# The division of a strip put ahead of the next strip's pass, the first loads reordered, the means of v behind the first scores

## The chip, the cores and the metric

One core of a Trainium2 chip runs the kernel. The metric is the device time of one execution in microseconds (us), the median of several runs.

## The reference

Windowed attention with block summaries, then two feed-forward layers on the same 1536 tokens (width 512, inner width 2048), all in float32.

```python
k_sum = k.reshape(B, H, nb, 32, D).max(axis=3)      # B=2 H=8 S=768 D=64 nb=24
v_sum = v.reshape(B, H, nb, 32, D).mean(axis=3)
scores_l = where(|i-j| < 16, scale * q @ k.T, -1e9)
scores_s = scale * einsum(q, k_sum) + log(32)
a = exp(concat(scores_l, scores_s) - rowmax)
a = a / (a.sum() + 1e-09)
x = a @ concat(v, v_sum)                             # -> 1536 x 512
g = max(h, 0) + alpha * min(h, 0),  h = x @ w_in     # layer 1
x = g @ w_out
g = P(h) / (Q(h) + 1e-6),  h = x @ w_in              # layer 2, P cubic, Q quadratic in |h|
out = g @ w_out
```

## The kernel before

The attention goes over 24 strips of 64 query rows (12 for each batch element). A strip needs 96 keys of its neighbourhood and 24 block maxima, so its score tile `s` is 128 x 4 x 120: two heads on the partitions, four head pairs beside each other. Its steps are small functions, and each has a short name in the tables below:

- `in` loads the strip's queries (`qz`, 256 KB), `v` its values (`vc`, 192 KB); `k` copies its keys out of the half of k that was loaded as a whole (`kt`) into `kc`; `ks` adds the block maxima `kmax`, `vm` the block means `vmean`.
- `qk` (line 394, TensorE) makes the scores; `mask` (402, VectorE) adds the bias, `max` (410, VectorE) finds the row extreme.
- `exp` (420, 424, ScalarE) has two forms, chosen for each strip by `SOFTMAX`: four activations that also add up the row ("a"), or one wide one ("s") after `sub` (415, GpSimd) with `sum` (429, VectorE) behind it.
- `guard` (434, 436) adds 1e-9 to the sum, `inv` (440, VectorE) takes the reciprocal, `norm` (444, VectorE or GpSimd) multiplies. `turn` (450, TensorE) transposes, `turned` copies the result `pT`, `pv` (464, TensorE) multiplies with the values into `po`, `out` and `outl` (478, VectorE) split `po` into a high part `xh` and a rest `xl`.

The feed-forward layers run each product as three TensorE passes of high and low parts (lines 195 and 258). Their weights come as raw words (`raw`, 1 MB each, two buffers) and are split by ScalarE (`top`, line 161), VectorE (`cv`, 163), ScalarE again (`wih`, `woh`) and GpSimd (`wil`, `wol`, line 173). Layer 1 of the first tokens starts while the attention still runs: its first product `h` is in pass 6 and needs strips 0 to 3.

The order is written out by hand. A loop over passes t = -1 to 27 (lines 576 to 622) goes through one of the strings in `ORDERS`; `PHASES = (3, 5, 7, 10, 14)` says which: the first for t < 3, the second for t = 3, 4, the third for 5, 6, the fourth for 7 to 9, the fifth for 10 to 13. In pass t `qk`, `mask` and `max` serve strip t, `exp`, `sum`, `guard`, `inv` and `norm` strip t-1, `turn` strip t-2, `pv` and `out` strip t-3, `k` strip t+1. Every engine works off its instructions strictly in that order. `ENG` names the engine of a step in each of the six phases (a ScalarE, v VectorE, p GpSimd). `FIRST` is the order of the loads before the loop. `VMEAN_AT` gives the pass in which each 128 rows of v enter the block means (`att_vmean`, line 359, TensorE, tile `vps`), `VLOAD_T` the pass from which the rows of the second batch element are loaded, `KMAX_AT` and `KLOAD_AT` the same for the block maxima and loads of k of the second element. All loads are issued by SyncE, in order; each waits until the load eight places ahead of it has landed, and where it fills a buffer again also for that buffer's readers. `na` and `ab` are the coefficients of layer 2.

From pass 10 on, and in all that follows, the order is not touched by the change.

Of the kernel before, what the change touches and what calls it, by code (L numbers as in the profile page):

```python
# [31 lines left out]
N_FIRST = 3  # L32
EARLY = 8

VMEAN_AT = (-1, -1, 0, 0, 1, 2, 6, 7, 8, 9, 9, 9)
VLOAD_T = 3
KMAX_AT = (3, 3, 3, 6, 9, 9, 9, 10)
KLOAD_AT = (2, 7)
WLOAD_AT = (1, 2)

PHASES = (3, 5, 7, 10, 14)
ORDERS = (
    ("qk mask k act mid exp max turn gl vmean sum kmax vm end ks out hi low pv inv sub outl Y norm guard turned "
     "v act in act H gh new"),
    ("act qk sum hi mid turn act vm act mask in exp vmean gh gl max pv ks v guard out inv sub low turned k end Y "
     "outl kmax H new norm"),
    ("qk vm exp hi act mask pv mid sum max out Y turn sub inv gl guard in low outl act v vmean k act norm H "
     "turned new ks end kmax gh"),
    ("gh qk act pv ks act act exp out end mask hi k sum gl max vmean outl low kmax turn guard mid Y v vm in sub "
     "inv new turned H norm"),  # L50
    ("ks act end act gh exp qk pv hi out mid v act mask k sum gl max outl sub turn vmean Y kmax low H turned in "
     "new inv vm guard norm"),
    ("vm act act gh act qk exp mask hi sum max pv gl inv sub out k mid v outl in turn turned vmean kmax new low "
     "guard ks Y end H norm"),
)

FIRST = 'k0 v0 v1 k1 q0 q2 v2 v3 q1'

SOFTMAX = 'aaaassasaasssabssssssass'

ENG = {"guard": "vapppv", "k": "vaaaaa", "turned": "aaaaaa", "vm": "aaapaa", "ks": "ppppav", "norm": "vppppp", "sub": "pppppp",
       "gl": "vvvppp", "gh": "vapaaa", "hi": "vaaaaa", "mid": "pvpppp", "end": "pppppp", "out": "aaaaaa", "al": "vavaaa"}

LEAD = (4, 6, 4, 4, 9, 13, 5, 10)
# [6 lines left out]
def kernel(  # L71
# [59 lines left out]
    def eng(step):  # L131
        return {"a": nc.scalar, "v": nc.vector, "p": nc.gpsimd}[ENG[step][sum(now[0] >= t for t in PHASES)]]

# [9 lines left out]
    def w_load(layer, nm, j):  # L143
        raw = rawp.tile([P, 4160], I16, tag="raw", name="raw")
        words = src_of[layer, nm][:, 2 * j:2 * j + 2, :].rearrange("p a b -> p (a b)").bitcast(I16)
        nc.sync.dma_start(out=raw[:, 1:4097], in_=words)
        raws[layer, nm, j] = raw
        loaded[layer, nm, j] = now[0]
# [32 lines left out]
    hps, ts, gs, yps, new, count = {}, {}, {}, {}, {}, [0]  # L181
# [51 lines left out]
    def g_split(u, f):  # L233
        n, t = u[3], ts[u, f]
        gh = gp.tile([P, 512], F32R, tag="gh", name="gh")[:, :n]
        gl = gp.tile([P, 512], F32R, tag="gl", name="gl")[:, :n]
        copy("gh", gh, t)
        gs[u, f] = gh, gl

    def g_low(u, f):  # L240
        t, (gh, gl) = ts.pop((u, f)), gs[u, f]
        (eng("gl") if (u, f) != steps[-1] else nc.vector).tensor_tensor(out=gl, in0=t, in1=gh.bitcast(F32), op=ALU.subtract)  # L242
# [66 lines left out]
    for e in range(3):  # L309
        t = a1.tile([P, KEYS], F32, name=f"bias{e}")  # L310
# [21 lines left out]
    kt, kmax, vt, vmean, st = {}, {}, {}, {}, {}  # L332

    def att_load(b, half):
        pool = e1 if (b, half) == (0, 1) else ktp
        kt[b, half] = pool.tile([P, NPAIR, HALF], F32, tag="kt", name="kt")
        for hp in range(NPAIR):
            nc.sync.dma_start(out=kt[b, half][:, hp, :], in_=kT[b, :, hp, half * (S // 2):half * (S // 2) + HALF])

    def att_kmax(b, i):  # L340
        half, hp = divmod(i, NPAIR)
        if i == 0:
            kmax[b] = a2.tile([P, NPAIR, NB], F32, tag="kmax", name="kmax")
        nc.vector.tensor_reduce(
            out=kmax[b][:, hp, half * NB // 2:(half + 1) * NB // 2],
            in_=kt[b, half][:, hp, WINDOW:WINDOW + S // 2].rearrange("p (n i) -> p n i", i=BLOCK),
            axis=AX.X, op=ALU.max)

    def att_vload(b, i):
        vt[b, i] = e1.tile([P, DM], F32, tag="vt", name="vt", bufs=NVT)  # L350
        s0 = WINDOW + i * P
        nc.sync.dma_start(out=vt[b, i], in_=vS[b, s0:s0 + P, :])

    def att_vmean(b, i):

        if i == 0:
            vmean[b] = psy.tile([P, 512], F32, tag=f"y{b}", name="vps")
        z0 = (NV - 1 - i) * (P // BLOCK)
        nc.tensor.matmul(out=vmean[b][0:KEYS, :], lhsT=mean[:, z0:z0 + KEYS], rhs=vt[b, i],
                         start=(i == 0), stop=(i == NV - 1))  # L360
        n = b * NV + i + NVT
        if n < B * NV:
            vlate.append(n)
        if i == NV - 1:
            ps, vmean[b] = vmean[b], (b1 if b else e1).tile([KEYS, DM], F32, tag=f"vmean{b}", name=f"vmean{b}")
            nc.scalar.copy(vmean[b][STRIP:KEYS, :], ps[STRIP:KEYS, :])
# [155 lines left out]
    def vmean_at(t):  # L522
        for i, at in enumerate(VMEAN_AT):
            if at == t:
                att_vmean(*divmod(i, NV))
        while vlate and (vlate[0] < NV or t >= VLOAD_T):
            att_vload(*divmod(vlate.pop(0), NV))

    def kmax_at(t):
        for i, at in enumerate(KMAX_AT):  # L530
            if at == t:
                att_kmax(1, i)
# [8 lines left out]
    def w_place(i):  # L541
        pool = ctx.enter_context(tc.tile_pool(name=f"wp{i}", bufs=1, reuse_waits="tile"))
        places.update({x: pool for x in opened[i][1]})

    def w_step(place, most=0):
        for i, (w, at, x) in enumerate(w_now):
            if at == place and (place != "hi" or x in places):
                w_now[i] = w, next(w, None), x
        w_now[:] = [x for x in w_now if x[1]]
        if len(w_now) < most and preps and preps[0] in raws and now[0] > loaded[preps[0]] + (now[0] <= LAST):  # L550
            layer, nm, j = p = preps[0]
            if now[0] >= need.get(p, 0) - LEAD[j] and now[0] + AHEAD >= opens[nm, j] and spare(*p):
                w = w_split(*preps.pop(0))
                w_now.append((w, next(w), (nm, j)))
# [13 lines left out]
    with tc.manual_schedule():  # L568
        for step in FIRST.split():
            {"k": lambda i: att_load(0, i), "v": lambda i: att_vload(0, i), "q": att_in}[step[0]](int(step[1]))  # L570
        for i in range(2 * NPAIR):
            att_kmax(0, i)
        for i, at in enumerate(VMEAN_AT):
            if at == -2:
                att_vmean(*divmod(i, NV))
        for t in range(-1, LAST + 1):
            now[0] = t
            if t == CLOSE_E:
                att_e.close()
                w_place(1)  # L580
            if t == NQ:
                att_qk.close()
                w_place(2)
            if t == 2:
                nc.sync.dma_start(out=al, in_=alpha)
                nc.sync.dma_start(out=na, in_=pa.partition_broadcast(P))
                nc.sync.dma_start(out=ab, in_=pb.partition_broadcast(P))
            if t == 5:
                nc.scalar.mul(na, na, -1.0)
                nc.scalar.activation(out=ab, in_=ab, func=AF.Abs)  # L590
            if t in KLOAD_AT:
                att_load(1, KLOAD_AT.index(t))
            act = acts.pop(0) if acts else iter(())
            g = later.pop(t, None)
            for step in ORDERS[sum(t >= at for at in PHASES)].split():
                if step in attn:
                    f, o = attn[step]
                    for n in {t + o, t + o - (o < -1)}:
                        if 0 <= n < NQ and n - t - o == -(o < -1 and n >= EARLY):
                            f(n)  # L600
                elif step in every:
                    every[step](t)
                elif step == "act":
                    next(act, None)
                elif step in ("gh", "gl"):
                    if g:
                        (g_split if step == "gh" else g_low)(*g)
                else:
                    w_step(step, 2 if step == "new" else 0)
            if t in WLOAD_AT:  # L610
                w_load(*loads.pop(0))
        for act in acts:
            for _ in act:
                pass
        for t in sorted(later):
            g_split(*later[t])
            g_low(*later[t])
# [104 lines left out]
```

## Time and profile before

| what | us |
|---|---|
| median of 3 runs | 621.86 (621.47 to 623.15) |
| the profiled execution, own time | 620.94 |
| its span | 618.8 |
| TensorE busy | 594.4 (96% of the span) |
| ScalarE, GpSimd, VectorE busy | 383.7, 354.8, 338.9 |

Some 2.1 us of the profiled execution lie outside its span. Rows of the trace give start, duration, engine, line, output, input, count, and in brackets how long the engine had been idle before and what released it. PEld are TensorE's weight loads, DVE is VectorE, ACT ScalarE, POOL GpSimd, SPq the queue of SyncE. Rows on one engine overlap by about 0.1 us, since an instruction starts while the one before it still writes.

### The profile page before, as it was taken

Reading aid. Unit: us, or ns where it says so; the run is one execution under the profiler, and the core shown is the slowest. Engines: PE = TensorE matmul, PEld = TensorE weight load, DVE = VectorE, ACT = ScalarE, POOL = GpSimd, SP = SyncE. Lnnn points to the kernel's source line nnn. Section 1 sums busy time; section 2 is a strip of 40 time slices with the busy share of each in tenths; the row PEclk is TensorE's granted clock in tenths of the full one; section 3 lists DMA queues with packets and bytes.
Section 4 is the critical chain, followed back from the end, with each engine's and each line's share of the span. In section 5 each row is a group of like instructions: output and inputs, shape, how many; then the busy total and the mean of one; then the engine's idle time right before and its main releaser. Section 6 shows DMA issues by size and latency. Waiting matters only on the chain.

```text
span 618.8 us, 8590 instructions
## 1 busy us (share of the span) xinstructions
PE 594.4 (96%) x3192; PEld 496.2 (80%) x3192; DVE 338.9 (55%) x494; ACT 383.7 (62%) x665; POOL 354.8 (57%) x343
## 2 busy tenths in 40 slices
PE   4679999999999999999999999999999999999996
PEld 2567989988888888888888888888888888888884
DVE  4766678654222111144555277776566666566664
ACT  1789798877444333367777467776566666566663
POOL 3266779675622222147777557776466666466662
PEclk9779999999999999999999999999999999999999
DMA  8898576524300000015555101000100000100001
GB/s 298 294 322 285 172 243 226 192 83 151 122 0 2 0 1 1 0 69 187 182 183 197 68 1 68 1 0 2 48 21 1 0 1 1 69 0 2 0 2 68
DMA packets 17129, 55.09 MB, mean 89 GB/s; under 512 B 2368, under 2 KB 4416, under 8 KB 12992
## 3 DMA queue, kind: packets, MB, share of 16 engines
q1 hardware_dynamic: 17088, 54.55, 26.1%
q8 instruction: 25, 0.41, 0.3%
q14 instruction: 16, 0.13, 0.1%
HBM read 51.39 MB, written 3.15 MB: 88 GB/s over the span
## 4 chain that ended last, share of the span: by engine, by line
PE 75%; DVE 10%; ACT 7%; DMA 3%; POOL 2%; issue 2%; SPq 1%; DVEq 0%; ACTq 0%
PE h L195 35%; PE y L258 35%; DVE tp L230 2%; DVE tp L220 2%; DVE h L229 2%; DVE tu L228 2%; ACT h L226 2%; ACT h L227 2%; PE s L394 1%; DVE tp L219 1%; PE po L464 1%; DMA na<-in_pa 1%; DMA raw<-in_w_in 1%; PE pt L450 1%; ACT top L161 1%
## 5 line engine op out<-in xcount | busy, mean ns | idle before, releaser
L195 PE MATMUL h<-xh,wih 128*128 128x512 f32 (+1 forms) x416 | 155.7, 374 | 0.0
L195 PE MATMUL h<-xl,wih 128*128 128x512 f32 (+1 forms) x416 | 155.2, 373 | 0.0
L195 PE MATMUL h<-xh,wil 128*128 128x512 f32 (+1 forms) x416 | 155.0, 373 | 0.0
L242 POOL TENSOR_TENSOR gl<-tp,gh 128x512 fp32r<-128x512 f32 (+1 forms) x75 | 95.2, 1269 | 80.3 <-ACT gh L137 78.9
L137 ACT ACTIVATE gh<-tp 128x512 fp32r<-128x512 f32 (+1 forms) x76 | 46.2, 608 | 91.6 <-DVE tp L230 46.0
L195 PEld LDWEIGHTS h<-xh,wih 128*128 128x128 f32 x416 | 78.3, 188 | 13.9 <-ACT kc L137 0.2
L195 PEld LDWEIGHTS h<-xl,wih 128*128 128x128 f32 x416 | 78.3, 188 | 14.0 <-issue 0.2
L195 PEld LDWEIGHTS h<-xh,wil 128*128 128x128 f32 x416 | 78.4, 188 | 13.8
L258 PE MATMUL y<-gh,woh 128*128 128x512 f32 (+1 forms) x224 | 81.9, 366 | 0.0
L258 PE MATMUL y<-gh,wol 128*128 128x512 f32 (+1 forms) x224 | 80.3, 359 | 0.0
L258 PE MATMUL y<-gl,woh 128*128 128x512 f32 (+1 forms) x224 | 80.3, 359 | 0.0
L258 PE MATMUL y<-woh,gh 128*128 128x512 f32 x192 | 74.8, 390 | 1.1 <-ACT gh L137 1.1
L163 DVE SCALAR_TENSOR_TENSOR cv<-raw,top 128x1024 int32<-128x1024 int32 x32 | 59.2, 1848 | 30.4 <-ACT top L161 23.9
L258 PE MATMUL y<-wol,gh 128*128 128x512 f32 x192 | 74.7, 389 | 0.0
L258 PE MATMUL y<-woh,gl 128*128 128x512 f32 x192 | 74.5, 389 | 0.0
L228 DVE SCALAR_TENSOR_TENSOR tu<-tu,h 128x512 f32<-128x512 f32 x48 | 33.0, 688 | 71.0 <-ACT h L227 67.5
L217 POOL TENSOR_SCALAR tu<-tv,ab 128x512 f32<-128x512 f32 x48 | 37.1, 774 | 58.0 <-ACT tv L215 58.0
L218 POOL TENSOR_TENSOR tu<-tu,tv 128x512 f32<-128x512 f32 x48 | 62.2, 1296 | 4.0
L242 POOL TENSOR_TENSOR gl<-tu,gh 128x512 fp32r<-128x512 f32 (+1 forms) x28 | 33.1, 1184 | 49.9 <-ACT gh L137 49.9
L208 DVE SCALAR_TENSOR_TENSOR tp<-h,tp 128x512 f32<-128x512 f32 (+1 forms) x28 | 17.2, 614 | 69.9 <-ACT tp L137 69.9
L226 ACT ACTIVATE h<-tu,lnb 128x512 f32<-128x512 f32 x48 | 33.2, 692 | 35.1 <-DVE tp L220 32.7
L208 DVE SCALAR_TENSOR_TENSOR tu<-h,tu 128x512 f32<-128x512 f32 (+1 forms) x28 | 17.2, 613 | 60.6 <-ACT tu L137 60.6
(79 smaller groups left out, 1061.4 us busy)
## 6 DMA issues: line engine op xcount, KB each, us to landing
raw<-in_w_in SPq DMA_DIRECT2D x16, 1024.0 KB, 4.8
raw<-in_w_out SPq DMA_DIRECT2D x16, 1024.0 KB, 4.8
qz<-in_qT SPq DMA_DIRECT2D x25, 256.0 KB, 5.3
vc<-in_vS SPq DMA_DIRECT2D x24, 192.0 KB, 5.4
kt<-in_kT SPq DMA_DIRECT2D x16, 208.0 KB, 5.4
vt<-in_vS SPq DMA_DIRECT2D x12, 256.0 KB, 5.1
out<-stage SPq DMA_DIRECT2D x12, 256.0 KB, 2.1
al<-in_alpha SPq DMA_DIRECT2D x1, 8.0 KB, 6.0
```

What stands on the lines that cost most here:

```text
L137: e.activation(out=out, in_=in_, func=AF.Copy, scale=1.0 if scale is None else scale)
L163: nc.vector.scalar_tensor_tensor(out=w.bitcast(I32), in0=rest, scalar=13, in1=top, op0=ALU.logical_shift_right, op1=ALU.bitwise_or)
L195: nc.tensor.matmul(out=ps, lhsT=a, rhs=b, start=(c == 0 and m == 0), stop=(c == NC - 1 and m == 2))
L208: nc.vector.scalar_tensor_tensor(out=t, in0=ps, scalar=0.0, in1=t, op0=ALU.max, op1=ALU.subtract)
L217: nc.gpsimd.tensor_scalar(out=q, in0=v, scalar1=ab[:, 1:2], scalar2=ab[:, 0:1], op0=ALU.mult, op1=ALU.add)
L218: nc.gpsimd.tensor_tensor(out=q, in0=q, in1=v, op=ALU.mult)
L220: nc.vector.scalar_tensor_tensor(out=p, in0=p, scalar=na[:, 1:2], in1=ps, op0=ALU.add, op1=ALU.mult)
L226: nc.scalar.activation(out=A, in_=q, func=AF.Ln, scale=2.0 ** -LN_SHIFT, bias=lnb)
L227: nc.scalar.activation(out=A, in_=A, func=AF.Exp, scale=-1.0, bias=exb)
L228: nc.vector.scalar_tensor_tensor(out=q, in0=q, scalar=one, in1=A, op0=ALU.add, op1=ALU.mult)
L242: (eng("gl") if (u, f) != steps[-1] else nc.vector).tensor_tensor(out=gl, in0=t, in1=gh.bitcast(F32), op=ALU.subtract)
L258: nc.tensor.matmul(out=yps[c][:, c0:c0 + n] if layer == 0 else yps[c], lhsT=a, rhs=b, start=(f == 0 and c0 == 0 and m == 0), stop=(f == NF ...
```

## The change

In the first four strings `guard inv norm` now stand in this order, right behind `exp` or `sum`, and ahead of `turn`; from the second string on that is also ahead of `mask` or `max`. `guard` moves from GpSimd to ScalarE in phases 2 and 3 (t = 5 to 9). In the first string `max` stands ahead of `k`, in the second `exp` ahead of `vm`. The block means of the first element enter two by two in passes 0, 1 and 2 (before: two pairs ahead of the first scores). Both halves of k are loaded first, one of two loads of the third strip's queries (q2) is left out, the loads of k and v for the second element come two and one pass later, and `na` and `ab` are loaded in pass 14 and prepared in pass 18 (before: 2 and 5).

```diff
-VMEAN_AT = (-1, -1, 0, 0, 1, 2, 6, 7, 8, 9, 9, 9)
-VLOAD_T = 3
-KMAX_AT = (3, 3, 3, 6, 9, 9, 9, 10)
-KLOAD_AT = (2, 7)
+VMEAN_AT = (0, 0, 1, 1, 2, 2, 6, 7, 8, 9, 9, 9)
+VLOAD_T = 4
+KMAX_AT = (6, 6, 7, 7, 9, 9, 10, 10)
+KLOAD_AT = (4, 7)
+PLOAD_AT = 14
...
-    ("qk vm exp hi act mask pv mid sum max out Y turn sub inv gl guard in low outl act v vmean k act norm H "
+    ("qk vm exp hi act sum guard inv norm mask pv mid max out Y turn sub gl in low outl act v vmean k act H "
...
-FIRST = 'k0 v0 v1 k1 q0 q2 v2 v3 q1'
+FIRST = 'k0 k1 q0 v0 v1 q1 v2 v3'
...
-ENG = {"guard": "vapppv",
+ENG = {"guard": "vaaapv",
...
             if t == 2:
                 nc.sync.dma_start(out=al, in_=alpha)
+            if t == PLOAD_AT:
                 nc.sync.dma_start(out=na, in_=pa.partition_broadcast(P))
                 nc.sync.dma_start(out=ab, in_=pb.partition_broadcast(P))
-            if t == 5:
+            if t == PLOAD_AT + 4:
```

TensorE at its start, before (`s` are the scores of strips 0, 1, 2, 3; `vps` the block means):

```order
L359 MATMUL vps_226<-vt_200,mean_187 120x512
L359 MATMUL vps_226<-vt_202,mean_187 120x512
L394 MATMUL s_235<-kc0_181,qz0_178 128x120 x4
L359 MATMUL vps_226<-vt_211,mean_187 120x512
L359 MATMUL vps_226<-vt_213,mean_187 120x512
L394 MATMUL s_251<-kc1_182,qz1_179 128x120 x4
L359 MATMUL vps_226<-vt_229,mean_187 120x512
L394 MATMUL s_282<-kc0_181,qz2_180 128x120 x4
L450 MATMUL pt_297<-ident_126,p_240 120x128 x4
L359 MATMUL vps_226<-vt_231,mean_187 120x512
L394 MATMUL s_314<-kc1_182,qz0_178 128x120 x4
```

And now:

```order
L395 MATMUL s_227<-kc0_181,qz0_178 128x120 x4
L360 MATMUL vps_238<-vt_206,mean_187 120x512
L360 MATMUL vps_238<-vt_208,mean_187 120x512
L395 MATMUL s_248<-kc1_182,qz1_179 128x120 x4
L360 MATMUL vps_238<-vt_211,mean_187 120x512
L360 MATMUL vps_238<-vt_213,mean_187 120x512
L395 MATMUL s_273<-kc0_181,qz2_180 128x120 x4
L451 MATMUL pt_291<-ident_126,p_232 120x128 x4
L360 MATMUL vps_238<-vt_241,mean_187 120x512
L360 MATMUL vps_238<-vt_243,mean_187 120x512
L395 MATMUL s_306<-kc1_182,qz0_178 128x120 x4
```

Between the scores of strips 0 and 3 stand six of these products where four stood, and none stands ahead of the scores of strip 0.

ScalarE in pass 3, before (`p_287` is strip 2, `xh` the first `out`):

```order
L366 COPY vmean0_303<-vps_226 24x512
L137 ACTIVATE pT_308<-pt_297 120x512
L137 ACTIVATE vc0_183<-vmean0_303 24x512
L424 ACTIVATE p_287,d_290<-p_287,m_289 128x120 x4
L434 ACTIVATE d_290<-d_290 128x4
L137 ACTIVATE xh_93<-po_343 128x4x64
L137 ACTIVATE pT_356<-pt_319 120x512
L137 ACTIVATE kc0_181<-kt_195 128x4x96
```

And now:

```order
L367 COPY vmean0_298<-vps_238 24x512
L138 ACTIVATE pT_300<-pt_291 120x512
L425 ACTIVATE p_278,d_281<-p_278,m_280 128x120 x4
L435 ACTIVATE d_281<-d_281 128x4
L138 ACTIVATE vc0_183<-vmean0_298 24x512
L138 ACTIVATE xh_93<-po_330 128x4x64
L138 ACTIVATE pT_341<-pt_318 120x512
L138 ACTIVATE kc0_181<-kt_195 128x4x96
```

The copy of the means into `vc` stood ahead of `exp` and now stands behind `guard`, next to the `xh` whose `po` needs it.

VectorE from the `max` of pass 6 to the reciprocal of pass 7, before (`d_427` and `d_473` are the sums of strips 5 and 6, `p_470` is strip 6, `xl` of `po_474` is strip 3):

```order
L402 SCALAR_TENSOR_TENSOR p_470<-s_460,bias1_147 128x480
L429 TENSOR_REDUCE d_427<-p_424 128x4
L410 TENSOR_REDUCE m_472<-p_470 128x4
L440 RECIPROCAL d_427<-d_427 128x4
L478 TENSOR_TENSOR xl_94<-po_474,xh_93 128x4x64
L344 TENSOR_REDUCE kmax_360<-kt_277 128x12
L208 SCALAR_TENSOR_TENSOR tu_532<-h_503,tu_532 128x256
L402 SCALAR_TENSOR_TENSOR p_550<-s_527,bias1_147 128x480
L410 TENSOR_REDUCE m_552<-p_550 128x4
L478 TENSOR_TENSOR xl_94<-po_534,xh_93 128x4x64
L163 SCALAR_TENSOR_TENSOR cv_518<-raw_403,top_91 128x1024
L440 RECIPROCAL d_473<-d_473 128x4
```

And now (the sums are `d_422` and `d_468`):

```order
L430 TENSOR_REDUCE d_422<-p_419 128x4
L441 RECIPROCAL d_422<-d_422 128x4
L403 SCALAR_TENSOR_TENSOR p_465<-s_451,bias1_147 128x480
L411 TENSOR_REDUCE m_467<-p_465 128x4
L479 TENSOR_TENSOR xl_94<-po_469,xh_93 128x4x64
L345 TENSOR_REDUCE kmax_512<-kt_347 128x12 x2
L209 SCALAR_TENSOR_TENSOR tu_525<-h_494,tu_525 128x256
L403 SCALAR_TENSOR_TENSOR p_543<-s_520,bias1_147 128x480
L441 RECIPROCAL d_468<-d_468 128x4
L411 TENSOR_REDUCE m_545<-p_543 128x4
L479 TENSOR_TENSOR xl_94<-po_527,xh_93 128x4x64
L164 SCALAR_TENSOR_TENSOR cv_509<-raw_397,top_91 128x1024
```

The reciprocal, which needs ScalarE's `guard`, moved from behind `max`, `xl` and `cv` to ahead of them.

## Rows read from the trace of the kernel before

**Rows 1.** The page's part 1: busy time, share of the span and instructions of each engine.

```profile
PE 594.4 (96%) x3192; PEld 496.2 (80%) x3192; DVE 338.9 (55%) x494; ACT 383.7 (62%) x665; POOL 354.8 (57%) x343
```

**Rows 2.** Busy time by stretches: length, PE, PEld, DVE, ACT, POOL, PEclk, DMA share, GB/s.

```profile
0.00:11.39 11.39, 3.35 (x4) 1.12 (x5) 5.58 (x10) 1.28 (x1) 5.60 (x35) 1.00 0.81 276
11.39:19.15 7.76, 7.22 (x37) 4.70 (x38) 5.15 (x12) 3.25 (x16) 0.15 (x1) 1.00 1.05 329
24.30:37.00 12.70, 9.38 (x61) 8.05 (x62) 7.89 (x13) 10.51 (x24) 4.74 (x5) 0.50 1.05 334
37.00:53.00 16.00, 13.21 (x124) 10.93 (x123) 9.88 (x20) 12.40 (x28) 11.05 (x14) 0.98 1.01 333
53.00:530.00 477.00, 475.48 (x2578) 401.23 (x2577) 253.09 (x357) 302.22 (x504) 283.92 (x248) 1.00 0.23 77
...
52.90:60.00 7.10, 7.10 (x55) 5.24 (x54) 5.47 (x11) 6.99 (x19) 5.69 (x7) 1.00 0.67 221
```

**Rows 3.** Timeline, TensorE's block means and the scores of strips 0, 3 and 4.

```profile
7.39 3.35 PE L359 MATMUL vps<-vt,mean 128*120 128x512 f32 x4 [7.39 <-DMA vt<-in_vS]
...
11.39 1.15 PE L394 MATMUL s<-kc,qz 128*128 128x120 f32 x8 [0.65 <-POOL kc L139]
...
12.45 1.98 PE L359 MATMUL vps<-vt,mean 128*120 128x512 f32 x4
...
19.15 1.05 PE L394 MATMUL s<-kc,qz 128*128 128x120 f32 x8
...
24.30 2.07 PE L394 MATMUL s<-kc,qz 128*128 128x120 f32 x8 [2.37 <-ACT kc L137]
```

**Rows 4.** Timeline, passes 3 and 4.

```profile
21.25 0.69 PE L464 MATMUL po<-pT,vc 120*64 120x64 f32 x16
...
22.87 0.21 ACT L434 ACTIVATE d<-d 128x4 f32<-128x4 f32 x1
```

**Rows 5.** A piece of the chain of waits: start, us, what.

```profile
24.07 7.23 DMA raw<-in_w_in
```

**Rows 6.** Timeline, ScalarE in pass 5.

```profile
31.38 1.35 ACT L161 ACTIVATE top<-raw 128x1024 f16<-128x1024 bf16 x1 [1.78 <-DMA raw<-in_w_in]
...
32.60 0.18 ACT L589 ACTIVATE na<-na 128x4 f32<-128x4 f32 x1
```

**Rows 7.** Timeline, passes 5 and 6, from the `exp` of strip 4 to the `xl` of strip 3.

```profile
33.53 0.60 ACT L420 ACTIVATE p<-p 128x480 f32<-128x480 f32 x1
...
36.39 1.97 POOL L415 TENSOR_TENSOR p<-p,m 128x480 f32<-128x480 f32 x1
...
37.88 0.66 DVE L402 SCALAR_TENSOR_TENSOR p<-s,bias 128x480 f32<-128x480 f32 x1
...
38.73 0.99 POOL L444 TENSOR_TENSOR p<-p,d 128x480 f32<-128x480 f32 x1
38.90 1.04 ACT L137 ACTIVATE wih<-cv 128x1024 fp32r<-128x1024 f32 x1
...
39.60 0.64 DVE L410 TENSOR_REDUCE m<-p 128x4 f32<-128x480 f32 x1
39.67 2.54 POOL L173 TENSOR_TENSOR wil<-cv,wih 128x512 fp32r<-128x512 f32 x2
...
40.16 0.17 DVE L440 RECIPROCAL d<-d 128x4 f32<-128x4 f32 x1
40.25 0.42 DVE L478 TENSOR_TENSOR xl<-po,xh 128x256 fp32r<-128x256 f32 x1
```

**Rows 8.** Timeline, pass 7 and the start of pass 8.

```profile
45.36 0.51 ACT L137 ACTIVATE kc<-kt 128x384 f32<-128x384 f32 x1
...
45.83 1.79 DVE L163 SCALAR_TENSOR_TENSOR cv<-raw,top 128x1024 int32<-128x1024 int32 x1
...
47.65 1.35 ACT L161 ACTIVATE top<-raw 128x1024 f16<-128x1024 bf16 x1 [1.78 <-DVE cv L163]
...
49.49 0.69 PE L464 MATMUL po<-pT,vc 120*64 120x64 f32 x16 [1.48 <-ACT pT L137]
```

More of the change, by code (lines that the diff above doesn't have):

```diff
@@ L33 @@
 EARLY = 8
-VMEAN_AT = (-1, -1, 0, 0, 1, 2, 6, 7, 8, 9, 9, 9)
-VLOAD_T = 3
-KMAX_AT = (3, 3, 3, 6, 9, 9, 9, 10)
-KLOAD_AT = (2, 7)
+VMEAN_AT = (0, 0, 1, 1, 2, 2, 6, 7, 8, 9, 9, 9)
+VLOAD_T = 4
+KMAX_AT = (6, 6, 7, 7, 9, 9, 10, 10)
+KLOAD_AT = (4, 7)
 WLOAD_AT = (1, 2)
+PLOAD_AT = 14
 PHASES = (3, 5, 7, 10, 14)
 ORDERS = (
[L43 to L46, printed above, removed]
-    ("qk vm exp hi act mask pv mid sum max out Y turn sub inv gl guard in low outl act v vmean k act norm H "
+    ("qk mask max k exp guard inv norm turn act mid act gl vmean sum kmax vm end ks out hi low pv sub outl Y "
+     "turned v in act H gh new"),
+    ("act qk exp sum hi mid guard inv norm turn act vm act mask in vmean gh gl max pv ks v out sub low turned k "
+     "end Y outl kmax H new"),
+    ("qk vm exp hi act sum guard inv norm mask pv mid max out Y turn sub gl in low outl act v vmean k act H "
      "turned new ks end kmax gh"),
-    ("gh qk act pv ks act act exp out end mask hi k sum gl max vmean outl low kmax turn guard mid Y v vm in sub "
-     "inv new turned H norm"),
+    ("gh qk act pv ks act act exp out end mask hi k sum guard inv gl norm max vmean outl low kmax turn mid Y v "
+     "vm in sub new turned H"),
     ("ks act end act gh exp qk pv hi out mid v act mask k sum gl max outl sub turn vmean Y kmax low H turned in "
@@ L55 @@
 )
-FIRST = 'k0 v0 v1 k1 q0 q2 v2 v3 q1'
+FIRST = 'k0 k1 q0 v0 v1 q1 v2 v3'
 SOFTMAX = 'aaaassasaasssabssssssass'
-ENG = {"guard": "vapppv", "k": "vaaaaa", "turned": "aaaaaa", "vm": "aaapaa", "ks": "ppppav", "norm": "vppppp", "sub": "pppppp",
+ENG = {"guard": "vaaapv", "k": "vaaaaa", "turned": "aaaaaa", "vm": "aaapaa", "ks": "ppppav", "norm": "vppppp", "sub": "pppppp",
        "gl": "vvvppp", "gh": "vapaaa", "hi": "vaaaaa", "mid": "pvpppp", "end": "pppppp", "out": "aaaaaa", "al": "vavaaa"}
```

## The prediction

> **What bounds the kernel now.** I read the page's busy times first: TensorE works in 96% of the span [rows 1]. The table by stretches says where the rest lies. From 53 to 530 us TensorE idles 1.5 us; before 53 it idles 11.39 - 3.35 = 8.0 us ahead of the first scores and 2.8 us between 37 and 53, and from 24.3 to 37 it idles 3.3 us and runs at half the clock (0.50, that is 1.2 of 2.4 GHz) [rows 2]. So the kernel has a head of some 53 us in which no engine is full, and behind it a row of products that TensorE works off without a hole. The change moves nothing behind pass 9, which ends at about 60 us. Whatever it gains or loses by then is shifted through to the end, one to one. The timeline of the head then shows what TensorE waits for: the block maxima (strip 0), `kc` from ScalarE (strip 4, 2.37 us) [rows 3], `pT` from ScalarE (`po`, 1.48 us) [rows 8]. These are chains through ScalarE, VectorE and GpSimd, each strictly in order, so the question is what the new order puts in front of what.
>
> The profiled execution took 620.94 us (span 618.8), 0.9 below the median of 621.86. I sum against 620.94 and add the 0.9 at the end.
>
> **The change, part by part.** Every + is later, every - earlier.
>
> *1. Both halves of k first.* Two loads of v (128 x 512 floats, 256 KB each) leave the front of the queue. At the 276 GB/s of this stretch [rows 2] that is 1.9 us at most for the last part of k; the reductions that follow and the load of q0, now right behind, keep some of it. I take -1.3 (between -0.5 and -1.9).
>
> *2. Means behind the scores.* Before, two of the six products of the means ran at 7.39 us, while TensorE waited for k anyway: free. They are also its first work. Four instructions took 3.35 us there and 1.98 us at 12.45 [rows 3], so the first ran at about half speed, though the granted clock reads 1.00 in that stretch [rows 2]; I go by the durations. Now the scores of strip 0 are the first work: 2.07 us, as at 24.30 under the granted 0.50, in place of 1.15 [rows 3], +0.9. Between the scores of strips 0 and 3 stand six products, not four: the first two between 1.98 (full clock) and 3.35 (low), I take 2.7; with 2 x 1.98 that is 6.7 against 2 x 1.98 before, +2.7. TensorE idled 7.76 - 7.22 = 0.5 in this stretch [rows 2], which takes up as much. Sum +3.1 (between +1.4 and +3.8): nothing hides it, since the products now stand in order ahead of the next scores. The Trainium skill (TensorE: Matmul & The Clock Gate, Part 1) says the throttled clock is the default state and that activity releases it, and warns there that the clock's trace events were seen to be unreliable. The column of this trace taken at its word would give the scores 1.15 and the two products 1.98, a sum 1.6 lower; the durations of rows 3 side with the page. At the scores of strip 3: +1.8.
>
> *3. `exp` ahead of `vm`, passes 3 and 4.* ScalarE's list is the same length, but `po` needs `vc`, and `xh` needs `po`. Before, `po` (0.69) ran at 21.25 beside `exp` [rows 4]; now `vc` ends just ahead of `xh`, and ScalarE waits for `po` with 0.1 of signals: +0.8 in each of the two passes (between 0, if ScalarE has slack there, and 1.2 with `po` at the low clock). Now +3.4. That VectorE's `mask` waits for `inv` costs nothing here: `mask` and `max` end while ScalarE copies `vc`, `xh`, `pT`, `kc`.
>
> *4. The second weights in time, pass 5.* SyncE waited for slots behind `na` and the second element's k; the second `raw` landed 7.23 us after 24.07 [rows 5], and ScalarE idled 1.78 us for it [rows 6]. Now that load stands ahead of those and follows the scores of strip 2, so it is issued some 4 us earlier and needed later. The wait goes, and so do two activations for `na` and `ab` (the row of one is 0.18, overlapped some 0.08 each): -1.9. They return in pass 18, inside a stretch where ScalarE is busy 302 of 477 us [rows 2]. `exp` of strip 4: +1.5.
>
> *5. Division ahead of `mask`, passes 5 and 6.* `guard` is on ScalarE now, behind `wih`. The new chain from `exp` of strip 4, each from rows 7 unless said: `exp` 0.60, `wih` 1.04, `guard` 0.21 [rows 4], `inv` 0.17, then on GpSimd `norm` 0.99 and the first half of `wil` 1.27 (which the new order leaves ahead of `sub`), `sub` 1.5 (1.97 in its row, where VectorE's `cv` ran beside; at least 1.0), `exp` 0.60, `wih` 1.04, `guard` 0.21, `inv` 0.17, `mask` 0.66, `max` 0.64, and then `xl`. That is 9.1, less the overlaps within engines, plus signals between them, 8.6. Before, the same way took 40.25 - 33.53 = 6.7 [rows 7]. +1.9 (between +0.5 and +2.5). The first `h` needs this `xl`. Now +3.4.
>
> *6. Pass 7.* `cv` (45.83) ran right behind `xl`; now `inv` waits for `guard`, which stands behind `kc` on ScalarE, and `max` follows. Ahead of `cv` come `kc` 0.51 [rows 8], `guard` 0.21, `inv` 0.17, `max` 0.64: 1.5, less overlaps +1.3. ScalarE already idled 1.78 for this `cv` ahead of `top`, and TensorE's `po` 1.48 for the `pT` behind `top` [rows 8], so all of it goes on (0 if `h` in between takes it up). Now +4.7.
>
> *7. `guard` on ScalarE, passes 8 and 9.* 0.21 each where ScalarE has no gap (6.99 busy of 7.10) [rows 2]: +0.4, at least 0.2. What GpSimd is spared there (`guard`) lies beside other work.
>
> The later loads for the second element cost nothing: k is asked for in pass 4 and reduced in pass 6, two passes on (from strip 3 to strip 4 alone it was 5.15 us [rows 3]), and even the 1 MB load of rows 5 landed in 7.23; one redundant 256 KB load of q less helps the queue. If they are late, VectorE stands still at `kmax` ahead of the first activation, and pass 7 grows by that.
>
> Sum: -1.3 +3.1 +1.6 -1.9 +1.9 +1.3 +0.4 = **+5.1 us**: 626.0 against the profiled execution, **626.9** against the median. With all low ends -1.9 +1.4 +0 -1.9 +0.5 +0 +0.2 = -1.7, with all high ends some +8.
>
> **The rivals.**
>
> *Faster: the loads are the head's clock.* From 11 to 53 us the DMA share is 1.01 to 1.05 in three stretches [rows 2]. If the strips follow the loads, the orders of ScalarE and VectorE cost nothing, and the gains alone count: -1.9 (k first), -1.9 (the wait for `raw`), and the 1.48 of `po` if the loads in pass 7 come forward too: -5.3, or 616.6 on the median's level; with a third of it given back in part 2, 618.5. Against it: ScalarE's waits name `cv`, not a load, in pass 7 [rows 8], and TensorE's wait at strip 4 names `kc` [rows 3]. It decides if the scores of strip 3 start before 19.2 us.
>
> *The same: TensorE is all that counts.* The Trainium skill (Perfetto Trace Analysis, Identifying Performance Opportunities) says that kernels are generally improved through the most-contended engine. By the rows that engine is TensorE at 96% [rows 1], its instructions are the same in number, and of the first 53 us it idles part in any order; gains and losses of the head would cancel within the 1.9 us (0.3%) that a measurement of this kernel can tell from no change, and the time would stay at 621.9. Against it: the idle time before 53 us is as long as I counted, so there is room to move it.
>
> *Slower still: the clock.* If TensorE's low clock, seen from 24.3 to 37 us [rows 2], comes earlier and lasts longer, parts 2 and 3 reach their high ends, +0.7 and +0.8, and a `po` or a product of the means at half speed on later chains adds up to the high sum: +6.6 to +8, or 628.5 to 629.9. Against it: the order leaves TensorE no longer hole there than before.
>
> **How the numbers follow.** My forecast, with the clock case in it, gets 0.66 for slower (0.58 and 0.08); the low ends of parts 2, 3 and 6 together with case two give 0.15 for no change; the first rival 0.19. The forecast's own range is 623.8 to 630. The range that leaves out 2 in 10 must reach into the first rival and up to the clock case: 619 to 630.5.
>
> **What would show it.** Right: scores of strip 0 at about 10 us and taking 2 us; of strip 3 near 21; ScalarE waiting for `po` ahead of `xh` in passes 3 and 4; no wait for `raw` in pass 5; the first `h` at 43 to 45 us (before, its last input ended at 40.25 + 0.42 [rows 7]), the `top` of pass 7 past 51; from there the same rows, shifted. Wrong: the scores of strip 3 before 19.2 us, or VectorE's `cv` in pass 7 before 46.5, or TensorE's rows behind 60 us not shifted by one amount.

## The result, and the profile after

The changed kernel takes **626.75 us** (median of 4 runs, 625.8 to 627.59), the kernel before, measured beside it, 621.66 (4 runs): ratio **1.0077, 95% interval 1.0053 to 1.0100**, slower by 4.8 us (the medians lie 5.1 apart). The forecast was 626.9. The profiled execution took 626.16 (span 624.3), 5.2 more than before's 620.94.

The work is the same; the page's busy times after, against [rows 1]:

```profile
PE 596.2 (96%) x3192; PEld 497.6 (80%) x3192; DVE 338.3 (54%) x494; ACT 384.4 (62%) x670; POOL 355.8 (57%) x338
```

TensorE is busy 1.8 us longer with the same 3192 instructions, so the rest of the 5.5 us of span is idle time. By stretches, columns as in [rows 2]:

```profile
0.00:11.00 11.00, 1.11 (x5) 1.11 (x6) 5.55 (x10) 1.28 (x1) 5.67 (x35) 1.00 0.81 269
...
24.00:28.00 4.00, 2.48 (x26) 2.34 (x27) 1.09 (x3) 3.29 (x9) 0.54 (x1) 0.82 1.02 367
...
32.00:37.00 5.00, 4.39 (x30) 3.69 (x31) 1.68 (x4) 4.95 (x9) 1.29 (x2) 0.52 1.07 339
37.00:45.00 8.00, 5.90 (x40) 4.18 (x40) 6.12 (x10) 4.90 (x9) 7.26 (x7) 0.79 0.85 298
45.00:53.00 8.00, 5.73 (x54) 4.82 (x52) 4.67 (x8) 4.67 (x15) 3.70 (x3) 1.00 0.77 224
53.00:60.00 7.00, 6.65 (x59) 5.21 (x59) 4.32 (x9) 5.87 (x16) 3.81 (x3) 0.76 0.54 197
```

From 37 to 53 us TensorE now idles 4.4 us (2.8 in [rows 2]), and from 53 to 60 the granted clock averages 0.76 where before had 1.00. The timeline of the head after shows where each microsecond came in:

```profile
9.89 2.06 PE L395 MATMUL s<-kc,qz 128*128 128x120 f32 x8 [9.89 <-POOL kc L140]
11.75 2.46 PE L360 MATMUL vps<-vt,mean 128*120 128x512 f32 x4
...
20.19 1.12 PE L395 MATMUL s<-kc,qz 128*128 128x120 f32 x8
...
24.69 0.38 ACT L138 ACTIVATE xh<-po 128x256 fp32r<-128x256 f32 x1 [0.79 <-PE po L465]
...
26.16 1.72 PE L395 MATMUL s<-kc,qz 128*128 128x120 f32 x8 [1.52 <-ACT kc L138]
...
30.93 0.39 ACT L138 ACTIVATE xh<-po 128x256 fp32r<-128x256 f32 x1 [1.22 <-PE po L465]
...
32.25 1.34 ACT L162 ACTIVATE top<-raw 128x1024 f16<-128x1024 bf16 x1
...
34.26 0.60 ACT L421 ACTIVATE p<-p 128x480 f32<-128x480 f32 x1
...
38.37 1.97 POOL L416 TENSOR_TENSOR p<-p,m 128x480 f32<-128x480 f32 x1
...
40.37 0.60 ACT L421 ACTIVATE p<-p 128x480 f32<-128x480 f32 x1 [2.55 <-POOL p L416]
...
43.39 0.42 DVE L479 TENSOR_TENSOR xl<-po,xh 128x256 fp32r<-128x256 f32 x1
...
49.67 1.80 DVE L164 SCALAR_TENSOR_TENSOR cv<-raw,top 128x1024 int32<-128x1024 int32 x1
...
51.51 1.35 ACT L162 ACTIVATE top<-raw 128x1024 f16<-128x1024 bf16 x1 [2.83 <-DVE cv L164]
```

And TensorE from the scores of strip 8 to those of strip 9, after:

```profile
49.68 1.04 PE L395 MATMUL s<-kc,qz 128*128 128x120 f32 x8
53.35 0.71 PE L465 MATMUL po<-pT,vc 120*64 120x64 f32 x16 [2.62 <-ACT pT L138]
53.99 2.06 PE L360 MATMUL vps<-vt,mean 128*120 128x512 f32 x2
55.85 1.06 PE L451 MATMUL pt<-ident,p 128*120 128x128 f32 x4
...
58.40 1.04 PE L395 MATMUL s<-kc,qz 128*128 128x120 f32 x8
```

The same rows before, behind the `po` with which [rows 8] end:

```profile
50.11 1.12 PE L359 MATMUL vps<-vt,mean 128*120 128x512 f32 x2
51.06 0.60 PE L450 MATMUL pt<-ident,p 128*120 128x128 f32 x4
...
52.93 1.04 PE L394 MATMUL s<-kc,qz 128*128 128x120 f32 x8
```

| what starts | before | after | later by | of it new |
|---|---|---|---|---|
| scores of strip 0 | 11.39 | 9.89 | -1.50 | -1.50 |
| scores of strip 3 | 19.15 | 20.19 | +1.04 | +2.54 |
| scores of strip 4 | 24.30 | 26.16 | +1.86 | +0.82 |
| scores of strip 5 | 29.66 | 32.39 | +2.73 | +0.87 |
| `exp` of strip 4 | 33.53 | 34.26 | +0.73 | -2.00 |
| `xl` of strip 3 | 40.25 | 43.39 | +3.14 | +2.41 |
| scores of strip 7 | 42.55 | 45.27 | +2.72 | -0.42 |
| `po` of strip 5 | 49.49 | 53.35 | +3.86 | +1.14 |
| scores of strip 9 | 52.93 | 58.40 | +5.47 | +1.61 |
| scores of strip 11 | 64.09 | 69.50 | +5.41 | -0.06 |

Behind strip 9 TensorE's rows are those of before, 5.4 us later (on VectorE, pass 10 takes over one `kmax` reduction of pass 9). The +1.61 at strip 9 is the piece that the sum did not hold: behind the 2.62 us in which TensorE stood idle (its hole) `vps` and `pt` take 2.06 and 1.06 us, where before had 1.12 and 0.60.

### The profile page after: what moved, and what is told of

The parts are those of the page before. It is cut to its first block, busy times and chain, and to the rows that moved or that the text cites. A ratio compares the mean times of both kernels' runs of the same rounds, so it can differ in the third digit from the quotient of the medians.

```text
span 624.3 us, 8592 instructions
## 1 busy us (share of the span) xinstructions
PE 596.2 (96%) x3192; PEld 497.6 (80%) x3192; DVE 338.3 (54%) x494; ACT 384.4 (62%) x670; POOL 355.8 (57%) x338
## 4 chain that ended last, share of the span: by engine, by line
PE 76%; DVE 10%; ACT 8%; POOL 2%; DMA 2%; issue 2%; SPq 1%; DVEq 0%; ACTq 0%; POOLq 0%
PE h L196 35%; PE y L259 34%; DVE tp L231 2%; PE s L395 2%; DVE tp L221 2%; DVE h L230 2%; DVE tu L229 2%; PE vps L360 2%; PE po L465 2%; ACT h L227 2%; ACT h L228 2%; DVE tp L220 1%; PE pt L451 1%; ACT top L162 1%; DMA qz<-in_qT 1%
```

## The experiments

The theory: the order costs some 5 us, the loads give about 2 back, the means behind the scores cost 2 to 3, and the low clock behind the hole in pass 8 is a price of its own. The rivals: the loads and means are the cause, or the clock of the head alone. "After" is the changed kernel with its 1.0077. Each ratio has an interval of 0.11% to 0.24% either way (0.7 to 1.5 us), and the difference of two is known only to some 1.4 to 2 us, so of the parts the trace tells more than the medians. Each experiment has one trace.

**1. The order undone, loads and means kept.** The four strings of the diff are set back, and

```diff
-ENG = {"guard": "vaaapv", "k": "vaaaaa", "turned": "aaaaaa", "vm": "aaapaa", "ks": "ppppav", "norm": "vppppp", "sub": "pppppp",
+ENG = {"guard": "vapppv", "k": "vaaaaa", "turned": "aaaaaa", "vm": "aaapaa", "ks": "ppppav", "norm": "vppppp", "sub": "pppppp",
```

> The changed kernel with the strings and the engine of guard of the kernel before; loads and means stay as changed. Theory (the order of exp, guard and inv in passes 3 to 9 costs the time, loads and means nearly nothing on balance): the scores of strip 3 stay near 20.2 us, ScalarE no longer waits for po in passes 3 and 4, no wait for the second raw, the first h near 40 us; 620.5 us, between 619.5 and 622. Rival (the later loads of the second element, or the means and the low clock, cost the time): it stays above 625.

Measured: 622.64 us (12 runs), ratio 0.9994 (0.9975 to 1.0013). Its timeline, TensorE:

```profile
19.82 1.12 PE L389 MATMUL s<-kc,qz 128*128 128x120 f32 x8
...
24.91 1.15 PE L389 MATMUL s<-kc,qz 128*128 128x120 f32 x8 [2.37 <-ACT kc L132]
...
48.00 0.69 PE L459 MATMUL po<-pT,vc 120*64 120x64 f32 x16 [1.49 <-ACT pT L132]
...
51.44 1.04 PE L389 MATMUL s<-kc,qz 128*128 128x120 f32 x8
```

The waits of before are back, 2.37 and 1.48 in [rows 3, 8]. The order is worth 1.0077 - 0.9994 = 0.83%, 5.2 us. Loads and means together are worth nothing that can be told from noise, as the sum had it (parts 1, 2 and 4: -0.1). The profiled execution, the fastest of the twelve with 619.26, is ahead of before's (strip 9 at 51.44, before 52.93).

**2. The order alone.** The changed strings and `guard` in the kernel before.

```diff
-ENG = {"guard": "vapppv", "k": "vaaaaa", "turned": "aaaaaa", "vm": "aaapaa", "ks": "ppppav", "norm": "vppppp", "sub": "pppppp",
+ENG = {"guard": "vaaapv", "k": "vaaaaa", "turned": "aaaaaa", "vm": "aaapaa", "ks": "ppppav", "norm": "vppppp", "sub": "pppppp",
```

> The kernel before with the strings and the engine of guard of the changed one; loads and means as before. Theory: two waits for po of 0.8 each, some 2.4 in passes 5 and 6, 1.7 in passes 7 to 9, less the 1.78 that ScalarE waited for raw and no longer does since it arrives later: +4.2, 626 us (625 to 627.5). Rival (loads and means cost the time): within 1.9 of 621.7.

Measured: 626.21 us (6 runs), ratio 1.0060 (1.0037 to 1.0083), 3.7 us; `po` of strip 5 at 53.39 behind a wait of 2.28, granted clock 0.76 from 53 to 60. `xh` waits for `po` 0.79 and 1.22, as in the changed kernel. There is no wait for `raw`. Experiments 1 and 2 agree that it is the order that costs the time: taken out, the loss is gone, and alone it brings most of it.

**3. The loads alone**: order and means of before, loads as changed but for the first: here both halves of k do not come first, so part 1 is not in it. From the changed kernel, beside the edits of experiment 1:

```diff
-VMEAN_AT = (0, 0, 1, 1, 2, 2, 6, 7, 8, 9, 9, 9)
+VMEAN_AT = (-1, -1, 0, 0, 1, 2, 6, 7, 8, 9, 9, 9)
-FIRST = 'k0 k1 q0 v0 v1 q1 v2 v3'
+FIRST = 'k0 v0 v1 k1 q0 q1 v2 v3'
```

> The order of before and its times for the means of v, with the loads of k, v and the parameters moved and the first steps as halves of k after the first two pieces of v. Theory (the second weights come in time when the loads are moved, worth up to 1.9 us in part 4): no wait of the top halves for raw, scores of strip 0 at 11.4 us with 1.15 us, scores of strip 4 at about 24.3 us, scores of strip 9 about 51.2 us (52.93 in before), ratio about 0.997 (0.995 to 0.999). Rival (the top halves wait for something else as soon as raw is there): scores of strip 9 at 52.5 us or later, ratio 0.999 to 1.001.

Measured: 620.74 us (6 runs), ratio **0.9963** (0.9949 to 0.9977), 2.3 us faster. The timeline, ScalarE's second `top` and TensorE's scores of strip 6:

```profile
29.53 1.36 ACT L156 ACTIVATE top<-raw 128x1024 f16<-128x1024 bf16 x1 [0.40 <-DVE cv L158]
...
33.85 2.06 PE L389 MATMUL s<-kc,qz 128*128 128x120 f32 x8
```

The 1.78 us wait for `raw` of [rows 6] is gone, and strip 6 starts at 33.85 (before 35.82). Strip 9 at 52.72 missed the 51.2 expected and lies where the rival had it, while the ratio is the theory's: in this execution the granted clock still averages 0.72 from 37 to 45 us (0.97 before), and `vps` takes 1.91 us there (before 1.02), which took most of it back in this trace; the median keeps the gain.

**4. The means early**, all else as changed (the edits of experiment 3 without those of 1, so parts 1 and 2 are both undone).

> The changed kernel with the means of v in the passes of the kernel before, and the first two loads of v between the halves of k again. Theory: scores of strip 0 near 11.2 us at 1.15, of strip 3 near 18.9 (changed kernel 20.19), and the 1.3 goes through to the end: 625.4 us (624.6 to 626.2). Rival (TensorE's low clock at the start is absorbed later, since ScalarE sets the pace from pass 3 on): 626.7, no change.

Measured: 625.58 us (8 runs), ratio 1.0047 (1.0029 to 1.0066). The median is as expected, the way to it is not: scores of strip 3 at 20.36, not 18.9. From strip 0 to strip 3 it takes 8.97 us, in experiment 3 with the old order 7.75: VectorE's `mask` rows stand 3.1 and 2.9 us apart there, against 2.8 and 2.4. So in these traces the first of the strings (passes 0 to 2) costs 1.2 us of its own, which the sum put at nothing; in the changed kernel most of it hides beside TensorE's products of the means. TensorE around its hole in this execution:

```profile
48.94 1.04 PE L395 MATMUL s<-kc,qz 128*128 128x120 f32 x8
...
52.27 0.69 PE L465 MATMUL po<-pT,vc 120*64 120x64 f32 x16 [2.28 <-ACT pT L138]
...
55.71 1.04 PE L395 MATMUL s<-kc,qz 128*128 128x120 f32 x8
```

The granted clock stays at 1.00 from 53 to 60: the low clock does not follow every such hole. From scores to scores it takes 6.77 us, 1.95 less than after; 0.34 of that is the shorter hole, the other 1.6 the clock.

**5. A warm start.** Ahead of the first step:

```diff
+        warm = ps_t.tile([P, 512], F32, tag="pt", name="warm")
+        for _ in range(4):
+            nc.tensor.matmul(out=warm, lhsT=ident, rhs=top.bitcast(F32)[:, 0:512], start=True, stop=True)
         for step in FIRST.split():
```

> The changed kernel with four products of 128 x 512 (eight instructions, of the identity with zeros, result unused) ahead of the first scores. Theory: TensorE is at full speed when k arrives, so the scores of strip 0 take 1.15 us in place of 2.06 and the first means 1.9 in place of 2.46: 1.4 us less at strip 1, some of it kept to the end: 625.5 us (624.8 to 626.5). If the first scores still take 2 us, the slow start does not come from what TensorE did before.

Measured: 625.55 us (6 runs), ratio 1.0050 (1.0030 to 1.0069), as expected. Scores of strip 0 at 9.49 take 1.15, `vps` behind them 1.88 in place of 2.46, strip 3 starts at 18.78 (after 20.19). TensorE's first work was slow for want of work ahead of it.

**6. Old order and warm start**, the edits of 1 and 5 together.

> The order of before with the changed loads and means, and four products 128x512 of the identity with zeros ahead of the first step. Theory (the order costs the time, the loads give it back, the slow start of TensorE eats part of the gain): scores of strip 0 at about 9.5 us taking 1.15 us instead of 2.06, scores of strip 3 at about 18.8 us (19.82 without the products), no wait of the top halves for raw, product with v of strip 5 behind a wait of about 1.5 us for pT; ratio about 0.997 (0.994 to 0.999), below the 0.9994 without the products. Rival (loads and means never reach the end, whatever the start): scores of strip 3 early, yet ratio 0.999 to 1.001.

Measured: 620.05 us (6 runs), ratio **0.9961** (0.9949 to 0.9973): as expected, and faster than both kernels. The timeline of TensorE:

```profile
9.42 1.15 PE L389 MATMUL s<-kc,qz 128*128 128x120 f32 x8 [1.49 <-POOL kc L134]
...
17.86 1.05 PE L389 MATMUL s<-kc,qz 128*128 128x120 f32 x8
```

Against experiment 1 it is 0.33% or 2.1 us faster, which is the price of the slow start (strip 3 at 17.86, in experiment 1 at 19.82). The 1.9 us between experiments 3 and 1 (0.9994 - 0.9963) are another sum: there the means go behind the scores and both halves of k come first, parts 1 and 2 together, which the prediction had at +1.8.

**7 to 9. One string set back at a time** in the changed kernel: the second (passes 3, 4), the third (5, 6) and the fourth (7 to 9), in the last two with `guard` of that phase on GpSimd. The fourth:

```diff
-    ("gh qk act pv ks act act exp out end mask hi k sum guard inv gl norm max vmean outl low kmax turn mid Y v "
-     "vm in sub new turned H"),
+    ("gh qk act pv ks act act exp out end mask hi k sum gl max vmean outl low kmax turn guard mid Y v vm in sub "
+     "inv new turned H norm"),
```

> The changed kernel with only the string of passes 3 and 4 set back (exp behind vm again, inv behind max). Theory: ScalarE's two waits for po (0.79 and 1.22 us in the changed kernel) go, strip 5 comes 1.7 us earlier and that goes through: 1.7 under the changed kernel, a ratio to the kernel before near 1.005 (1.003 to 1.006). Rival (GpSimd sets the pace in passes 5 and 6, so what ScalarE gains is waited away there): no change, 1.008.

Measured: 625.24 us (8 runs), ratio 1.0042 (1.0028 to 1.0056), as expected; no wait of `xh` for `po`; strip 4 to strip 5 takes 4.96 us (after 6.23, before 5.36).

> The changed kernel with only the string of passes 5 and 6 and the engine of guard in them set back. Theory: from exp of strip 4 to xl of strip 3 it takes 6.7 us again in place of 9.1, so 2.4 under the changed kernel: a ratio to the kernel before near 1.004 (1.002 to 1.005). Rival (those passes only hide behind what passes 7 to 9 cost): ratio 1.007 or more.

Measured: 625.29 us (5 runs), ratio 1.0049 (1.0030 to 1.0069), just inside; `xl` of strip 3 at 40.99 (after 43.39), but strip 7 at 44.82 (after 45.27). Of the 2.4 us most does not come through: TensorE's `pt` starts at 40.51, behind GpSimd's `norm`, and a `vps` of 1.91 us at the low clock follows. Both run at nearly the same time after (40.76, 1.92 us), but there they lie beside the wait for `xl`.

> The changed kernel with only the string of passes 7 to 9 and the engine of guard in them set back. Theory: cv of pass 7 right behind xl, the hole of TensorE ahead of po some 1.5 us in place of 2.6; 0.7 for the chain, 0.4 for guard, and, if the hole is then too short for the clock to fall, 1.6 more: 1.1 to 2.7 under the changed kernel, ratio to the kernel before 1.0035 to 1.006, and a granted clock of 1.00 from 53 to 60 us in the profile. Rival (passes 7 to 9 are bound by ScalarE anyway): ratio 1.0075.

Measured: 624.57 us (11 runs), ratio 1.0029 (1.0018 to 1.0040), below the range expected; the granted clock is 1.00 from 53 to 60, as expected. The timeline of TensorE:

```profile
50.91 1.05 PE L389 MATMUL s<-kc,qz 128*128 128x120 f32 x8
...
52.88 0.69 PE L459 MATMUL po<-pT,vc 120*64 120x64 f32 x16 [0.93 <-ACT pT L132]
...
56.33 1.04 PE L389 MATMUL s<-kc,qz 128*128 128x120 f32 x8
```

The hole is 0.93, and strip 8 to strip 9 takes 5.42 us against 8.72 after: by the traces this string is the dearest. The three undone parts are worth 2.2, 1.7 and 3.0 us, 6.9 together where the whole order is worth 5.2. Each of these is uncertain by 1.6 to 1.9 us, so that they do not add up is not shown.

**10. The fourth string alone.** Experiment 1 with that string as changed and `guard` on ScalarE in its phase.

> The order of before in all passes but 7 to 9, which keep the changed string and the guard on ScalarE; loads and means as changed. Theory (the string of passes 7 to 9 costs some 3 us by itself, about half of it by the low clock behind its hole): wait of TensorE for pT ahead of the product with v of strip 5 of 2.3 to 2.7 us, scores of strip 8 to those of strip 9 8.0 to 8.8 us, ratio 1.003 to 1.005, against 0.9994 with the old order throughout. Rival (its cost shows only behind the later head that the other strings make): wait of 1.5 to 1.8 us, 6 to 6.5 us between the scores, ratio 0.999 to 1.001.

Measured: 624.06 us (12 runs, 620.18 to 624.97), ratio 1.0017 (1.0002 to 1.0032): below the 1.003 to 1.005 of the theory, and 1.4 us above experiment 1, which is no more than the uncertainty of that difference. The trace agrees with the theory:

```profile
48.73 1.05 PE L389 MATMUL s<-kc,qz 128*128 128x120 f32 x8
...
52.03 0.69 PE L459 MATMUL po<-pT,vc 120*64 120x64 f32 x16 [2.25 <-ACT pT L132]
...
57.06 1.04 PE L389 MATMUL s<-kc,qz 128*128 128x120 f32 x8
```

The clock is 0.76 from 53 to 60, and from scores to scores it takes 8.33 us (5.97 in experiment 1). Nine of the twelve executions, the profiled one among them, took 623.7 us or more at a mean granted clock of 0.983 to 0.986, the other three 622.4 or less at 0.991 to 0.993. The mechanism stands in this one trace; its size in the median is about half of what was expected and not clear of noise.

**11, 12. Products in the hole.** Behind the scores of strip 8 of the changed kernel, eight products (and in another run sixteen) that nothing reads:

```diff
                              start=True, stop=True)
+        if n == 8:
+            fill = ps_o.tile([P, NPAIR, QS], F32, tag="po", name="fill")
+            for _ in range(8):
+                nc.tensor.matmul(out=fill[:, 0:2, :], lhsT=ident, rhs=ident, start=True, stop=True)
         st[n] = s
```

> The changed kernel with eight products 128x128 of the identity with itself behind the scores of strip 8 (half as many as in the longer filling, so some 1.9 us, inside the hole of 2.6 us). Theory (the low granted clock behind the hole costs about 1.6 us): from the scores of strip 8 to those of strip 9 about 7.1 us (8.72 in the changed kernel, 8.17 with the long filling), granted clock 1.00 from 53 to 60 us, ratio about 1.005. Rival (the low clock there hides under other waits): 8.5 to 8.7 us between the scores, ratio 1.007 to 1.008.

Measured with eight: 625.43 us (6 runs), ratio 1.0049 (1.0037 to 1.0061). TensorE's timeline, and the stretch:

```profile
50.29 1.05 PE L395 MATMUL s<-kc,qz 128*128 128x120 f32 x8
51.17 1.96 PE L400 MATMUL fill<-ident 128*128 128x128 f32 x16
53.98 0.69 PE L469 MATMUL po<-pT,vc 120*64 120x64 f32 x16 [0.85 <-ACT pT L138]
...
57.42 1.04 PE L395 MATMUL s<-kc,qz 128*128 128x120 f32 x8
```

```profile
53.00:60.00 7.00, 6.15 (x62) 4.74 (x61) 4.26 (x10) 6.93 (x21) 3.19 (x3) 1.00 0.61 215
```

From scores to scores 7.13 us (7.1 expected, 8.72 without), clock 1.00: work added to the busiest engine shortens this stretch by 1.6 us, and the ratio lies 0.28% or 1.7 us under the changed kernel's, with about as much uncertainty. One rival stays: in this execution the low clock lasted longer already before the added products could act (0.53 from 37 to 45, after 0.79), and the mean granted clock of the six executions, 0.982 to 0.989, is no higher than the changed kernel's 0.981 to 0.988. So it is not proved that the products alone kept the clock up behind the hole.

> The changed kernel with 16 small products of the identity with itself (128 x 128, result unused) behind the scores of strip 8, where TensorE has its hole of 2.6 us. Nothing that other engines wait for moves. Theory: the hole takes 1.6 us beyond its own length because TensorE runs at half speed behind it, so with it filled the granted clock stays at 1.00 from 53 to 58 us, strip 9 starts 1.6 us earlier, ratio to the kernel before 1.005 to 1.006. Rival (the low clock there is a matter of the run, or ScalarE binds anyway): ratio 1.0075 to 1.008.

Measured with sixteen: 626.82 us (5 runs), ratio 1.0067 (1.0050 to 1.0085), above the range. They took 3.74 us, longer than the hole, so `po` came some 1 us late; the clock did stay at 1.00.

## Why the prediction was right

The total was right to 0.2 us, and so was the side of every part but part 7. That it came so close is luck: in the traces the seven parts of the sum gave +3.8 us where it had +5.1, and a piece that was not in it gave +1.6. Of the signs that it named, two were missed by little: strip 3 at 20.19, not near 21, and the first `h` at 42.59, not 43 to 45.

- *Parts 1 and 4, the loads, -1.3 and -1.9.* In the trace of the changed kernel -1.50 and -2.00. Part 4 without part 1 is experiment 3: -2.3 in the median, by the wait for `raw` that is gone.
- *Part 2, the means, +3.1.* +2.54 in this trace. The scores took 2.06 as said, and 1.15 with work ahead of them (experiments 5 and 6). The rule of the Trainium skill (TensorE: Matmul & The Clock Gate, Part 1), that the throttled clock is the default state, agrees. The six products took 2.46, 1.88 and 1.88, together 6.2 where the sum had 6.7. The first pair is what moves: in the eight traces that start so (the changed kernel, experiments 1 and 7 to 12) it takes 2.46 to 3.62 us, and from strip 0 to strip 3 it is 10.27 to 11.53, against 7.76 before. That is +2.5 to +3.8, with the forecast in the middle; this trace lies at the low end.
- *Part 3, `exp` ahead of `vm`, +0.8 twice.* +0.82 and +0.87, with the waits for `po` in both places.
- *Part 5, +1.9.* +2.41 at `xl`, of which 0.42 is gone again at the scores of strip 7, so +1.99. ScalarE idles 2.55 us for `sub`, which took 1.97, again beside VectorE's `cv`, and not the 1.5 of the sum.
- *Part 6, +1.3.* +1.14: the hole ahead of `po` grew from 1.48 [rows 8] to 2.62.
- *Part 7, +0.4.* Nothing: from strip 9 to strip 11 the distance is that of before, 11.1 us.
- *Not in the sum: the clock behind the hole, +1.6.* Against the clock rival the prediction said "the order leaves TensorE no longer hole there than before". Up to 37 us, the stretch that it spoke of, that holds (longest hole 1.74, ahead of the `po` at 23.96; before 2.37). As a reason to leave the clock out of the sum it failed: part 6 of the same sum lengthens a hole at 50 us, and in this trace the low clock came behind that one. Of the seven traces with a hole of 2.25 to 2.63 us there, six have the low clock behind it (the changed kernel, experiments 2, 5, 7, 8 and 10) and one has not (4). Of the seven with 1.49 or less, or with products in it, none has.
- *The rivals.* Loads as the head's clock: strip 3 started at 20.19, later than the 19.2 from which that decides, and the order alone (experiment 2) loses 3.7 us with the loads as before. TensorE is all that counts: with the same 3192 instructions the order is worth 3.7 to 5.2 us, so the share of 96% hid a head in which no engine bounds. That rival came from the Trainium skill (Perfetto Trace Analysis, Identifying Performance Opportunities), by which kernels are generally improved through the most-contended engine; the share of the whole span did not show which engine that is in these 53 us.

Taken one after the other (before, experiment 3, experiment 1, the changed kernel), the moved loads cost -2.3 us, both halves of k first together with the means +1.9, and the order +5.2, where the sum had -1.9, +1.8 and +5.2. Each is uncertain by 1 to 2 us. In the trace of the changed kernel the order is made up otherwise than forecast: its parts give 4.8 and the clock 1.6, together 6.4, which that uncertainty covers. How much of that 1.6 is in the medians stays open, since the executions of before have much the same mean granted clock (0.982 to 0.993) as those of the changed kernel (0.981 to 0.988).

## What to carry to other kernels

Where one engine is full but for its first stretch, read that stretch strip by strip: what an order puts ahead of a split or a copy there can be paid to the end, however idle the engines look in the totals. Before an in-order engine is given a step earlier, list what stands behind it and who waits for that; and if the chain ends in a hole of TensorE, reckon with the low clock for the work behind the hole as well, since a hole that grows may bring it. A change of several pieces can hold a gain inside a loss: the later loads alone (experiment 3) are faster than before. Loads that nothing needs yet belong behind those that are waited for, and first work on TensorE is cheapest when it is work of no consequence.

## What the runs showed of the hardware

- The granted-clock column reads 1.00 from 0 to 11 us after, while the eight products of the first scores took 2.06 us; behind four unread products they took 1.15 (experiments 5 and 6). Durations tell the level at the start, the column does not.
- A hole of 2.62 us on TensorE was followed by the clock at half (mean 0.76 from 53 to 60, `vps` 2.06 in place of 1.12). Holes of 2.25 to 2.63 at this place were so in experiments 2, 5, 7, 8 and 10 (0.76 to 0.83); in experiment 4 one of 2.28 was not, nor were those of 1.48 before and 0.93 in experiment 9. What decides was not settled.
- One kernel's executions differ by up to 4.8 us. In some kernels that goes with the mean granted clock: experiment 1 gave 619.26 us at 0.994 and 623.98 at 0.982. In others it does not: experiment 9 gave 624.1 to 624.8 at 0.989 and 623.3 to 624.7 at 0.983 to 0.986. Where the low clock lies in the head differs from trace to trace (24 to 48 us: 0.57 in experiment 9, 0.72 after, 0.86 in experiment 1), and one profile shows one such case.
